# A gated recurrence with a small expert layer on one Trainium2 core: r and k of five early tiles loaded as two 48-row halves onto zeroed buffers

## The chip, the cores and the metric

The kernel runs on one core of a Trainium2 chip. The metric is the device time of one execution in microseconds. Three runs of the kernel before took 87.02, 87.03 and 86.26 us, median 87.02 us.

## The reference

Two layers follow each other. The first is a linear recurrence over 768 steps for 4 x 8 heads of dimension 48; the second is a mixture of eight low-rank experts with the two best chosen for each token, added to its input.

```python
batch, n_heads, seq, head_dim = (4, 8, 768, 48)
for t in range(S):
    cur = einsum('bhd,bhe->bhde', u * kt, vt)
    y[:, :, t] = einsum('bhd,bhde->bhe', rt, state + cur)
    state = wt[:, :, :, None] * state + einsum('bhd,bhe->bhde', kt, vt)

# x = y as (4*768, 384); E = 8 experts of rank 16, K = 2
logits = x @ w_gate
w = softmax over the two largest logits
delta = sum over the two chosen e of  w_e * ((x @ A[e]) @ B[e])
return x + delta
```

## The kernel before

The 768 steps of each batch entry are cut into 6 chunks of 128 (`L`), which gives 24 tiles (`NT`); a tile holds all eight heads of 128 steps. Heads go in pairs `p` (four pairs, `P`): on the 128 partitions one head of a pair has partitions 0 to 47 and the other 64 to 111, with the 48 channels of a head as rows and the 128 steps of each pair as columns.

Partitions 48 to 63 and 112 to 127 are left over by this. The host fills them with **doubled rows**: 16 channels each of the last pair's two heads, once in each of the first three pairs' blocks. The product r\*k for the term with `u` is therefore formed over three blocks (`PQ` = 3, 384 columns) and already holds all four pairs; three matmuls with the table `ub` (line 284, `dgmm`) sum it to one number for each step and head.

For one tile the steps are: `load_rk` (line 192) loads r and k of the tile in one transfer of 128 rows of 1028 f32 into one of 12 buffers `rks`; `load_w` loads the decays of two tiles (tiles 0 and 1 one each), `load_v` the values (the first three tiles through SP and a cast, `castv`; the later ones through POOL's queue, converted to bf16 on the way). `ln` (ACT) takes the logarithm of w, `cs` (PE) its running sum with a triangular matrix, `expp` and `expm` (ACT) the two exponentials. `qmul` (POOL) is r\*k, `rmul` (POOL) is r times the growing decay, `kmul` (DVE, for some tiles POOL) k times its inverse. `amm` (PE) forms the 128 x 128 products of each head, `aev` (DVE) masks them, `ktr`/`ktev` turn k, `kv`, `resc` and `sev` carry the state, `dgmm` and `dv` make the term with `u`, and `ymd`, `ymS`, `ymv` add the three parts of y. Every three tiles the gate runs (`zl`, `top`, `gexp`, `gsel`, `gmul`, `gnorm`, `gmul2`, `zw`, `zT`, `zTev`), and each tile ends with `dmm`, `oev` and `store`.

Nothing is scheduled automatically: the string `ORDER` (line 53) lists every step of every tile, and each engine executes its own steps in the order of that list. SP issues the plain loads and the stores in the order of the list, and a transfer that must wait holds all later ones back. The tuples above it (`K_ON_POOL`, `KT_ON_DVE`, `S_ON_DVE`, `Y_ON_DVE`, `OUT_ON_DVE`, `ZT_ON_ACT`, `CAST_ON_ACT`, `V_ON_ACT`) say which engine does a step for which tile. `warm.n` is n matmuls on zeros that keep PE occupied at the beginning. Ahead of the list DVE clears the padded buffers `lws` (four) and `dvs` (three), and POOL builds three constant matrices.

The list begins (line 54):

```python
warm.5 load_w.0 load_rk.0 ln.0 cs.0 warm.4 expp.0 expm.0 rmul.0 kmul.0 amm.0 warm.1 aev.0 qmul.0 load_w.1
ln.1 cs.1 warm.2 expp.1 expm.1 load_v.0 castv.0 consts.0 castc.0 dgmm.0 warm.2 dv.0 ymd.0 load_rk.1 qmul.1
rmul.1 kmul.1 load_w.2 ln.2 ktr.0 warm.2 ktev.0 cs.2 expp.2 expm.2 dgmm.1 load_v.1 castv.1 castv.2 dv.1
load_v.3 load_rk.2 qmul.2 rmul.2 kmul.2 load_rk.3 qmul.3 load_w.4 amm.1 aev.1 ymv.0 yev.0 ktr.1 ktev.1 kv.0
```

Tiles 6 to 8 stand in it on POOL as `qmul.6`, `rmul.6`, `qmul.7`, `load_v.9`, `qmul.8`, `rmul.7`, `kmul.7`, `qmul.9`.

Of the kernel before, what the change touches and what calls it, by code (L numbers as in the profile page):

```python
# [55 lines left out]
rmul.1 kmul.1 load_w.2 ln.2 ktr.0 warm.2 ktev.0 cs.2 expp.2 expm.2 dgmm.1 load_v.1 castv.1 castv.2 dv.1
load_v.3 load_rk.2 qmul.2 rmul.2 kmul.2 load_rk.3 qmul.3 load_w.4 amm.1 aev.1 ymv.0 yev.0 ktr.1 ktev.1 kv.0
warm.3 sev.0 cs.3 expp.3 expm.3 dgmm.2 load_v.6 kv.1 resc.1 sev.1 ln.4 ymd.1 ymS.1 ymv.1 yev.1 amm.2 warm.1
kmul.3 cs.4 expp.4 expm.4 dv.2 ymd.2 aev.2 rmul.3 ktr.2 ktev.2 consts.1 castc.1 load_rk.4 qmul.4 rmul.4
kmul.4 load_rk.5 load_w.6 load_rk.6 ymS.2 ymv.2 yev.2 amm.3 aev.3 kv.2 sev.2 dgmm.3 dv.3 cs.5 expp.5 expm.5  # L60
rmul.5 kmul.5 zl.2 top.2 gsel.2 consts.2 amm.4 warm.2 aev.4 ktr.3 ktev.3 ymd.3 ymS.3 ln.6 qmul.5 gexp.2
gmul.2 qmul.6 kv.3 resc.3 ymv.3 yev.3 dgmm.4 dv.4 sev.3 gnorm.2 gmul2.2 cs.6 expp.6 expm.6 rmul.6 amm.5
load_rk.7 qmul.7 load_w.8 load_rk.8 load_rk.9 load_w.10 load_rk.10 load_rk.11 load_w.12 load_rk.12
load_rk.13 load_w.14 ktr.4 ktev.4 ymd.4 ymS.4 ymv.4 yev.4 load_v.9 kv.4 sev.4 dgmm.5 qmul.8 load_rk.14
load_rk.15 kmul.6 cs.7 expp.7 expm.7 rmul.7 kmul.7 zw.2 zT.2 ln.8 castc.2 dv.5 ymd.5 dgmm.6 ymS.5 warm.1
# [10 lines left out]
dmm.6 oev.6 ymv.12 yev.12 kv.12 sev.12 rmul.13 kmul.13 amm.13 load_v.18 ktr.13 ktev.13 dmm.8 oev.8 qmul.15
load_w.16 load_rk.16 ln.16 qmul.16 load_rk.17 zl.11 kmul.14 cs.15 expp.15 aev.13 ymd.13 top.11 gexp.11
gsel.11 dgmm.14 dv.14 ymS.13 rmul.14 kv.13 resc.13 gmul.11 gnorm.11 expm.15 rmul.15 ymv.13 yev.13 amm.14
aev.14 sev.13 ktr.14 ktev.14 cs.16 ymd.14 ymS.14 dgmm.15 ymv.14 gmul2.11 zw.11 kv.14 zT.11 kmul.15 amm.15
dv.15 ktr.15 expp.16 expm.16 rmul.16 kmul.16 yev.14 ymd.15 qmul.17 zTev.11 cs.17 store.3 sev.14 ymS.15  # L80
aev.15 ktev.15 dgmm.16 dv.16 load_w.18 load_rk.18 ln.18 qmul.18 load_rk.19 dmm.10 oev.10 expp.17 rmul.17
expm.17 ymv.15 yev.15 kv.15 resc.15 sev.15 amm.16 ktr.16 ktev.16 cs.18 expp.18 expm.18 aev.16 store.5 zl.14
top.14 gexp.14 ymd.16 dgmm.17 dv.17 dmm.9 oev.9 ymS.16 kmul.17 amm.17 load_w.20 load_rk.20 load_rk.21
qmul.19 ymv.16 yev.16 kv.16 sev.16 gsel.14 ln.20 kmul.18 gmul.14 gnorm.14 gmul2.14 aev.17 dgmm.18 dmm.11
oev.11 cs.19 expp.19 expm.19 ymd.17 ymS.17 ymv.17 zw.14 zT.14 store.6 rmul.18 amm.18 zTev.14 qmul.20 store.7
dv.18 ktr.18 ktev.18 yev.17 aev.18 rmul.19 kmul.19 load_w.22 load_rk.22 load_rk.23 cs.20 ymd.18 dmm.13
oev.13 store.8 store.10 dgmm.19 dv.19 expp.20 expm.20 rmul.20 kmul.20 dmm.12 oev.12 qmul.21 kv.18 sev.18
ln.22 ymv.18 yev.18 zl.17 top.17 gexp.17 gsel.17 gmul.17 qmul.22 amm.19 aev.19 gnorm.17 gmul2.17 ktr.19
ktev.19 cs.21 expp.21 expm.21 kmul.21 dmm.14 oev.14 ymd.19 rmul.21 dgmm.20 dv.20 qmul.23 ymS.19 zw.17 ymv.19
yev.19 kv.19 resc.19 sev.19 amm.20 cs.22 store.13 zT.17 zTev.17 ymd.20 store.12 ktr.20 ktev.20 expp.22  # L90
# [13 lines left out]
def tile_kernel(ctx: ExitStack, tc: tile.TileContext, rk, w, v, ublk, aw, bm, out):  # L104
    nc = tc.nc
    nc.scalar.preload_act_table_set("natural_log_exp_and_others")
    const = ctx.enter_context(tc.tile_pool(name="const", bufs=1))
# [19 lines left out]
    lws = []  # L127
    for i in range(NLW):
        t_ = const.tile([128, WL, H, 64], FP16, name=f"lw{i}")
        nc.vector.memset(t_, 0.0)  # L130
# [60 lines left out]

    def load_rk(t):
        o = rks[t % RING]
        nc.sync.dma_start(out=o, in_=rk[t])
# [62 lines left out]
    def qmul(t):  # L257
        q = wk.tile([128, PQ, L], BF16, name="q", bufs=3)
        (nc.vector if t in Q_ON_DVE else nc.gpsimd).tensor_mul(q, st[t]["r"][:, 0:PQ], st[t]["k"][:, 0:PQ])  # L259
# [300 lines left out]
    stages = (warm, load_w, load_rk, load_v, castv, consts, castc, ln, cs, expp, expm, qmul, rmul, kmul, ktr, dgmm, ktev, dv, amm,  # L560
              aev, aev2, kv, resc, sev, ymd, ymS, ymv, ymv2, yev, yev2, zl, zl2, zx, nmax, top, gexp, gsel, gmul, gnorm, gmul2, zw, zT, zTev, pick, xev, dmm,
              oev, oev2, store, store2)
# [62 lines left out]
```

## Time and profile before

| | |
|---|---|
| three runs, median (lowest to highest) | 87.02 us (86.26 to 87.03) |
| the profiled execution, its own time | 86.5 us |
| its span, first to last instruction | 84.7 us |
| mean granted TensorE clock | 0.999 |
| moved by DMA | 25.43 MB, mean 300 GB/s |
| r and k of one tile | one transfer of 514.0 KB, median 10.1 us from issue to landing |

The profile describes one execution. Its page gives the busy time of each engine (PE for matmuls, PEld for their weight loads, DVE, ACT, POOL, and SP for issuing), then the span in 40 equal slices of 2.1 us with the busy tenths of each engine and the DMA engines' share and rate, then the chain of work that ended last, followed back from the end, and the costliest groups of instructions. In rows of the timeline the numbers are the start, the length, and in brackets the idle time of that engine just before, with what ended it. Lines such as L264 are lines of the kernel before.

### The profile page before, as it was taken

The numbers are of one execution on the slowest core, as the hardware profiler recorded it, in microseconds if no ns is written. First come the engines' busy times: TensorE is split into PE (matmuls) and PEld (weight loads), VectorE is DVE, ScalarE is ACT, GpSimd is POOL, SyncE is SP. The second block draws the span as 40 slices with busy tenths as digits, with TensorE's granted clock in tenths as the row PEclk, the third lists the DMA queues.
The fourth block names the chain that finished last, engine by engine and source line by source line (L and its number), as shares of the span: only waits on it lengthen the run. The fifth ranks groups of instructions, "written<-read, shape, count | busy, mean of one in ns | idle before, by whom it ended". The sixth has DMA issues, their size and how long they took to land.

```text
span 84.7 us, 3422 instructions
## 1 busy us (share of the span) xinstructions
PE 74.1 (88%) x1359; PEld 56.2 (66%) x1363; DVE 71.9 (85%) x174; ACT 68.4 (81%) x151; POOL 66.8 (79%) x95
## 2 busy tenths in 40 slices
PE   4899988997697999999999999999989999998610
PEld 1325666684476978688887978788768789675500
DVE  5947689968879999999999999999989986995730
ACT  6274689782899999999999999998999899956510
POOL 6059899969697999999999999997997996902000
PEclk9999999999999999999999999999999999999999
DMA  1999999999999999999999999999989004604261
GB/s 24 333 368 384 391 409 413 295 328 318 421 410 413 400 292 388 392 278 293 398 415 402 414 337 254 373 410 402 415 334 328 27 0 143 226 33 167 93 231 51
DMA packets 10384, 25.43 MB, mean 300 GB/s; under 512 B 1280, under 2 KB 4992, under 8 KB 10368
## 3 DMA queue, kind: packets, MB, share of 16 engines
q1 hardware_dynamic: 9648, 23.15, 71.1%
q0 software_dynamic: 720, 2.06, 12.3%
q8 instruction: 10, 0.16, 0.7%
q14 instruction: 6, 0.05, 0.2%
HBM read 22.56 MB, written 4.72 MB: 322 GB/s over the span
## 4 chain that ended last, share of the span: by engine, by line
DMA 39%; PE 27%; DVE 16%; ACT 4%; issue 3%; POOL 3%; SPq 1%; DVEq 0%; POOLq 0%
DMA rk<-in_rk_dram 15%; DMA out_dram<-res 10%; DMA aw_f<-in_aw_dram 9%; DMA v_f<-in_v_dram 5%; DVE at L315 5%; PE a_ps L308 4%; PE kd L282 3%; PE y_ps L365 3%; PE x_ps L241 2%; DVE dv L300 2%; PE d_ps L535 2%; PE y_ps L372 2%; PE d_ps L519 2%; PE z_ps L407 2%; PE y_ps L356 2%
## 5 line engine op out<-in xcount | busy, mean ns | idle before, releaser
L264 POOL TENSOR_TENSOR rd<-rk,ep 128x512 bf16<-128x512 f32 x24 | 26.1, 1089 | 3.6 <-ACT ep L249 2.8
L315 DVE TENSOR_TENSOR at<-a_ps,mask 128x1024 bf16<-128x1024 f32 x23 | 27.9, 1215 | 0.7 <-PE a_ps L308 0.6
L259 POOL TENSOR_TENSOR q<-rk 128x384 bf16<-128x384 f32 x24 | 20.6, 864 | 1.1 <-DMA rk<-in_rk_dram 0.9
L249 ACT ACTIVATE ep<-x_ps 128x512 f32<-128x512 f32 x24 | 14.7, 615 | 3.6 <-PE x_ps L243 2.1
L171 ACT CAST xT<-y_ps 128x512 bf16<-128x512 f32 x22 | 13.2, 598 | 2.1 <-PE y_ps L372 1.8
L241 PE MATMUL x_ps<-tri,lw 128*128 128x128 f16 x96 | 11.6, 223 | 1.4 <-ACT lw L231 1.4
L300 DVE TENSOR_TENSOR dv<-v_bf,kd 128x384 bf16<-128x384 bf16 x21 | 11.4, 544 | 1.2 <-DMA v_bf<-in_v_dram 1.1
L231 ACT ACTIVATE lw<-w_in 128x768 f16<-128x768 f32 (+1 forms) x13 | 10.5, 811 | 2.2 <-DMA w_in<-in_w_dram 2.2
L241 PEld LDWEIGHTS <-lw 128*128 128x128 f16 x96 | 7.7, 99 | 3.4 <-ACT lw L231 2.8
L356 PE MATMUL y_ps<-ident,dv 128*128 128x128 bf16 x94 | 9.2, 219 | 0.4 <-DVE dv L300 0.3
L171 ACT COPY ks<-kd 128x384 bf16<-128x384 bf16 x16 | 7.9, 496 | 1.6 <-DVE df L442 1.4
L165 PE MATMUL idle_ps<-zero 128*128 128x512 bf16 x19 | 7.3, 499 | 1.5 <-DVE zero L112 1.2
L171 ACT COPY res<-d_ps 128x384 f32<-128x384 f32 x17 | 8.3, 495 | 0.1
L372 PE MATMUL y_ps<-at,v_bf 128*48 128x128 bf16 x160 | 8.0, 221 | 0.1
L535 PE MATMUL d_ps<-b_b,zT 128*128 128x384 bf16 x24 | 7.8, 327 | 0.3 <-DVE zT L169 0.3
L365 PE MATMUL y_ps<-rd,sb 48*48 48x128 bf16 x156 | 8.0, 220 | 0.0
L255 ACT ACTIVATE x_ps<-x_ps 128x512 f32<-128x512 f32 x13 | 8.0, 616 | 0.0
L519 PE MATMUL d_ps<-ident,xT 128*128 128x96 bf16 x92 | 7.7, 206 | 0.0
L356 PEld LDWEIGHTS <-dv 128*128 128x128 bf16 x96 | 6.4, 98 | 1.4 <-DVE dv L300 1.2
L407 PE MATMUL z_ps<-aw_b,xT 128*128 128x136 bf16 x92 | 6.8, 223 | 0.4 <-ACT res L171 0.4
L255 ACT ACTIVATE em<-x_ps 128x512 f32<-128x512 f32 x11 | 6.7, 610 | 0.0
L243 PE MATMUL x_ps<-ones,lw 128*128 128x128 f16 x48 | 6.6, 219 | 0.0
(188 smaller groups left out, 162.8 us busy)
## 6 DMA issues: line engine op xcount, KB each, us to landing
rk<-in_rk_dram SPq DMA_DIRECT2D x24, 514.0 KB, 10.1
out_dram<-res SPq DMA_DIRECT2D x23, 192.0 KB, 3.0
w_in<-in_w_dram SPq DMA_DIRECT2D x11, 384.0 KB, 10.2
v_bf<-in_v_dram POOLq DMA_DIRECT2D x2, 576.0 KB, 9.1
v_bf<-in_v_dram POOLq DMA_DIRECT2D x3, 288.0 KB, 7.9
w_in<-in_w_dram SPq DMA_DIRECT2D x2, 192.0 KB, 3.3
v_f<-in_v_dram SPq DMA_DIRECT2D x1, 384.0 KB, 5.8
aw_f<-in_aw_dram SPq DMA_DIRECT2D x1, 272.0 KB, 7.7
```

What stands on the lines that cost most here:

```text
L171: nc.scalar.copy(out=o, in_=i)
L231: nc.scalar.activation(out=lw[:, o:o + n, :, 0:D].rearrange("p c h d -> p (c h) d"), in_=w_in[:, 0:n].rearrange("p c (h d) -> p (c h) d", ...
L241: nc.tensor.matmul(x_ps[:, p, :], lhsT=lwof(t, p), rhs=tri, start=True, stop=t % WL == 0)
L249: nc.scalar.activation(out=ep[:, :, o + 1:o + L + 1], in_=st[t]["x"], func=ACT.Exp)
L255: nc.scalar.activation(out=em, in_=st[t]["x"], func=ACT.Exp, scale=-1.0)
L259: (nc.vector if t in Q_ON_DVE else nc.gpsimd).tensor_mul(q, st[t]["r"][:, 0:PQ], st[t]["k"][:, 0:PQ])
L264: (nc.vector if t in R_ON_DVE else nc.gpsimd).tensor_mul(rd, st[t]["r"], st[t]["ep"][:, :, 0:L])
L300: nc.vector.tensor_mul(o[:, :, 0:D], vseq[t], dg.to_broadcast([128, H, D]))
L315: nc.vector.tensor_mul(at.rearrange("s g p f -> s (g p) f"), st[t]["a_ps"].rearrange("s g p f -> s (g p) f"), mask.to_broadcast([128, H, L]))
L356: nc.tensor.matmul(st[t]["y"][p], lhsT=st[t]["dv"][:, 2 * p:2 * p + 2, :].rearrange("p a b -> p (a b)"), rhs=ident, start=(p == 0 or (t == ...
L365: nc.tensor.matmul(st[t]["y"][p][s_], lhsT=st[t - 1]["sb"][s_, p, :], rhs=st[t]["rd"][s_, p, :], start=False, stop=False, skip_group_check ...
L372: nc.tensor.matmul(st[t]["y"][p][g * 64:g * 64 + D], lhsT=vseq[t][:, h, :], rhs=at, start=False, stop=(h >= H - 2 or (t == NT - 1 and h % ...
```

## The change

For tiles 1 to 5 (`EARLY`) r and k are loaded without the doubled rows: two transfers of 48 rows, to partitions 0 to 47 and 64 to 111. The rows between them are cleared once by a new step `rz` (a memset of the whole buffer, on POOL for tiles 1, 4 and 5, on DVE for 2 and 3), so that they hold zeros; the buffers are used again by tiles 13 to 17 with full rows. For these tiles `qmul` takes four blocks of 128 columns and `dgmm` four matmuls, with a second set of four blocks in the table `ub`. The memsets of `lws` and `dvs` become steps of the list (`lz`, `dz`). The casts of v for tiles 1 and 2 and of the table `aw` move from POOL to ACT, other steps change between DVE and ACT, and the whole list is planned anew.

```diff
-CAST_ON_ACT = (2,)
-V_ON_ACT = ()
+CAST_ON_ACT = (1, 2)
+V_ON_ACT = (1, 2)
+EARLY = (1, 2, 3, 4, 5)
+RZ_ON_POOL = (1, 4, 5)
 K_ON_POOL = (5, 7, 9, 11, 13, 15, 17, 19, 21, 22, 23)
-KT_ON_DVE = (0, 2, 9, 10)
-S_ON_DVE = (1, 3, 6)
-Y_ON_DVE = (17,)
-OUT_ON_DVE = (1, 6, 10, 13, 16, 19, 23)
-ZT_ON_ACT = (11, 14, 17, 20)
+KT_ON_DVE = (0, 2, 7, 10, 12, 18, 20)
+S_ON_DVE = (3, 15)
+Y_ON_DVE = ()
+OUT_ON_DVE = (1, 7, 16, 17, 23)
+ZT_ON_ACT = (8, 14, 17, 20)

 ORDER = """
+warm.5 load_w.0 lz.3 rz.1 load_rk.0 rz.4 lz.0 lz.1 load_w.1 ln.0 dz.2 rz.3 dz.1 dz.0 cs.0 warm.4 expp.0
+expm.0 rmul.0 kmul.0 amm.0 rz.5 rz.2 consts.0 qmul.0 lz.2 aev.0 castc.0 ln.1 cs.1 warm.2 expp.1 expm.1
+load_v.0 castv.0 dgmm.0 warm.3 dv.0 load_rk.1 qmul.1 kmul.1 load_w.2 ln.2 ktr.0 ymd.0 cs.2 load_v.1 castv.1
+expp.2 expm.2 ktev.0 kv.0 dgmm.1 warm.2 sev.0 castv.2 load_v.3 dv.1 ktr.1 ktev.1 rmul.1 amm.1 load_rk.2
+qmul.2 rmul.2 kmul.2 load_rk.3 load_w.4 load_v.6 aev.1 ymv.0 yev.0 cs.3 dgmm.2 dv.2 ymd.1 qmul.3 expp.3
+expm.3 rmul.3 kmul.3 ln.4 ymS.1 ymv.1 yev.1 kv.1 resc.1 sev.1 ktr.2 amm.2 cs.4 expp.4 expm.4 ymd.2 ymS.2
+consts.1 castc.1 aev.2 ymv.2 amm.3 yev.2 ktev.2 kv.2 sev.2 dgmm.3 load_rk.4 qmul.4 rmul.4 kmul.4 load_rk.5
+cs.5 qmul.5 expm.5 zl.2 aev.3 amm.4 dv.3 ktr.3 expp.5 top.2 gsel.2 ymd.3 ymS.3 aev.4 load_w.6 load_rk.6 ln.6
+cs.6 kmul.5 gexp.2 gmul.2 gnorm.2 ktev.3 dgmm.4 dv.4 expp.6 ymv.3 yev.3 kv.3 resc.3 sev.3 rmul.5 amm.5
+gmul2.2 zw.2 expm.6 kmul.6 ktr.4 ktev.4 qmul.6 rmul.6 load_v.9 ymd.4 ymS.4 dgmm.5 dv.5 load_rk.7 load_w.8
+load_rk.8 ln.8 qmul.8 ymv.4 yev.4 kv.4 sev.4 qmul.7 consts.2 cs.7 aev.5 zT.2 ymd.5 dgmm.6 ymS.5 expm.7 dv.6
+zTev.2 amm.6 aev.6 ymv.5 ktr.6 expp.7 rmul.7 cs.8 castc.2 dmm.1 oev.1 dmm.0 yev.5 ymd.6 ktev.6 dgmm.7 dv.7
...

     for i in range(NLW):
         t_ = const.tile([128, WL, H, 64], FP16, name=f"lw{i}")
-        nc.vector.memset(t_, 0.0)
         lws.append(t_)
...
         t_ = const.tile([128, H, 64], BF16, name=f"dv{i}")
-        nc.vector.memset(t_, 0.0)
...
-    ub_f = const.tile([128, PQ, H], F32, name="ub_f")
-    ub = const.tile([128, PQ, H], BF16, name="ub")
+    ub_f = const.tile([128, PQ + P, H], F32, name="ub_f")
+    ub = const.tile([128, PQ + P, H], BF16, name="ub")
...
+    def lz(i):
+        nc.vector.memset(lws[i], 0.0)
+
+    def dz(i):
+        nc.vector.memset(dvs[i], 0.0)
+
+    def rz(t):
+        (nc.gpsimd if t in RZ_ON_POOL else nc.vector).memset(rks[t], 0.0)
+
     def load_rk(t):
         o = rks[t % RING]
-        nc.sync.dma_start(out=o, in_=rk[t])
+        if t in EARLY:
+            for i in (0, 64):
+                nc.sync.dma_start(out=o[i:i + D], in_=rk[t, i:i + D])
+        else:
+            nc.sync.dma_start(out=o, in_=rk[t])
...
     def qmul(t):
-        q = wk.tile([128, PQ, L], BF16, name="q", bufs=3)
-        (nc.vector if t in Q_ON_DVE else nc.gpsimd).tensor_mul(q, st[t]["r"][:, 0:PQ], st[t]["k"][:, 0:PQ])
+        n = P if t in EARLY else PQ
+        q = wk.tile([128, P, L], BF16, name="q", bufs=3)[:, 0:n]
+        (nc.vector if t in Q_ON_DVE else nc.gpsimd).tensor_mul(q, st[t]["r"][:, 0:n], st[t]["k"][:, 0:n])
...
-        for p in range(PQ):
-            nc.tensor.matmul(dg, lhsT=st[t]["q"][:, p, :], rhs=ub[:, p, :], start=(p == 0), stop=(p == PQ - 1))
+        n, o = (P, PQ) if t in EARLY else (PQ, 0)
+        for p in range(n):
+            nc.tensor.matmul(dg, lhsT=st[t]["q"][:, p, :], rhs=ub[:, o + p, :], start=(p == 0), stop=(p == n - 1))
...
+    for j in range(H):
+        ublk[j % 2, 0:D, PQ + j // 2, j] = u[j]
```

More of the change, by code (lines that the diff above doesn't have):

```diff
@@ L56 @@
[L56 to L65, printed above, removed]
@@ L76 @@
[L76 to L85, printed above, removed]
@@ L86 @@
[L86 to L90, printed above, removed]
@@ new lines @@
+amm.12 aev.12 zT.8 rmul.13 qmul.14 expm.13 kmul.13 cs.14 ktr.12 ktev.12 yev.11 ymd.12 zTev.8 dmm.7 oev.7
+expp.14 expm.14 rmul.14 kmul.14 load_w.16 load_rk.16 ln.16 load_rk.17 load_w.18 load_rk.18 dmm.6 oev.6
+load_v.18 ymv.12 yev.12 kv.12 sev.12 dgmm.13 dv.13 qmul.16 zl.11 top.11 gexp.11 gsel.11 gmul.11 qmul.15
+store.5 amm.13 aev.13 ktr.13 ktev.13 cs.15 expp.15 expm.15 rmul.15 ymd.13 dmm.8 dgmm.14 dv.14 gnorm.11
+ymS.13 kv.13 oev.8 ymv.13 yev.13 store.3 resc.13 sev.13 amm.14 aev.14 ktr.14 ktev.14 store.4 cs.16 expp.16
@@ new lines @@
+expm.16 store.6 ymd.14 ymS.14 gmul2.11 zw.11 dgmm.15 dv.15 load_rk.19 load_w.20 load_rk.20 load_rk.21
+load_w.22 kmul.15 qmul.18 ymv.14 yev.14 kmul.16 store.7 kv.14 zT.11 zTev.11 store.8 ln.18 amm.15 aev.15
+ktr.15 ktev.15 rmul.16 ymd.15 cs.17 dmm.10 dgmm.16 dv.16 qmul.17 sev.14 kv.15 ymS.15 resc.15 sev.15 amm.16
+aev.16 expm.17 kmul.17 ymv.15 ktr.16 expp.17 cs.18 oev.10 zl.14 top.14 yev.15 ymd.16 ktev.16 dgmm.17 dv.17
+rmul.17 gsel.14 expp.18 expm.18 rmul.18 kmul.18 gexp.14 gmul.14 gnorm.14 gmul2.14 dmm.9 oev.9 store.10
@@ new lines @@
+load_rk.22 load_rk.23 qmul.19 ymS.16 kv.16 sev.16 ymv.16 yev.16 amm.17 aev.17 ln.20 dgmm.18 dv.18 qmul.21
+dmm.11 oev.11 store.11 cs.19 expp.19 expm.19 rmul.19 kmul.19 ymd.17 ymS.17 amm.18 ymv.17 yev.17 zw.14 ktr.18
+ktev.18 aev.18 zT.14 zTev.14 qmul.20 cs.20 expp.20 expm.20 rmul.20 dgmm.19 dv.19 ymd.18 kmul.20 dmm.13
+oev.13 store.13 dmm.12 oev.12 store.12 kv.18 sev.18 ymv.18 yev.18 amm.19 aev.19 ktr.19 zl.17 top.17 gsel.17
+cs.21 ymd.19 ktev.19 dgmm.20 dv.20 ln.22 qmul.22 ymS.19 gexp.17 gmul.17 gnorm.17 gmul2.17 expp.21 rmul.21
@@ L558, in store2 @@
         nc.sync.dma_start(out=out[t * 128:(t + 1) * 128, HD // 2:], in_=st[t]["res"][:, HD // 2:])
[L560 removed]
+    stages = (lz, dz, rz, warm, load_w, load_rk, load_v, castv, consts, castc, ln, cs, expp, expm, qmul, rmul, kmul, ktr, dgmm, ktev, dv, amm,
               aev, aev2, kv, resc, sev, ymd, ymS, ymv, ymv2, yev, yev2, zl, zl2, zx, nmax, top, gexp, gsel, gmul, gnorm, gmul2, zw, zT, zTev, pick, xev, dmm,
```

44 lines of the change are left out of this document (21 added, 23 removed).

## The prediction, made before the change was run

> **What bounds the kernel now.** I read the page first (shares, slices, chain, transfers), then the stages, then the chain in order of time, and last POOL's own timeline, because the page shows two different kernels in one: a beginning that waits for transfers and a long middle in which every engine is full.
>
> ```profile
> span 84.7 us, 3422 instructions
> PE 74.1 (88%) x1359; PEld 56.2 (66%) x1363; DVE 71.9 (85%) x174; ACT 68.4 (81%) x151; POOL 66.8 (79%) x95
> ...
> POOL 6059899969697999999999999997997996902000
> ...
> DMA  1999999999999999999999999999989004604261
> GB/s 24 333 368 384 391 409 413 295 328 318 421 410 413 400 292 388 392 278 293 398 415 402 414 337 254 373 410 402 415 334 328 27 0 143 226 33 167 93 231 51
> ...
> DMA 39%; PE 27%; DVE 16%; ACT 4%; issue 3%; POOL 3%; SPq 1%; DVEq 0%; POOLq 0%
> ```
>
> The 16 DMA engines are full from the second slice (2.1 us each) to about 64 us. POOL has holes up to slice 13 and none for long after it. The stages say the same in numbers; the columns are the length, then busy time of PE, PEld, DVE, ACT and POOL, the clock, the DMA share and GB/s.
>
> ```profile
> 5.00:10.00 5.00, 4.55 (x44) 2.18 (x42) 3.51 (x5) 2.98 (x6) 4.57 (x7) 1.00 1.01 390
> 10.00:27.00 17.00, 14.15 (x274) 10.74 (x275) 14.09 (x28) 13.41 (x28) 14.93 (x20) 1.00 1.04 375
> 27.00:57.00 30.00, 29.79 (x617) 24.67 (x613) 29.39 (x71) 29.61 (x69) 29.77 (x37) 1.00 1.04 361
> 57.00:75.00 18.00, 17.38 (x358) 14.03 (x351) 16.68 (x40) 15.95 (x39) 15.46 (x21) 1.00 0.61 226
> 75.00:84.70 9.70, 4.76 (x80) 3.33 (x74) 4.78 (x20) 4.04 (x11) 0.44 (x2) 0.99 0.35 123
> ```
>
> From 10 to 27 us DVE, ACT and POOL each lose 2 to 3.6 us; from 27 to 57 us none of them loses even 0.7 us. The chain and POOL's timeline (start, length, in brackets the idle time before and its releaser) show where the one regime turns into the other.
>
> ```profile
> 2.11 4.14 DMA v_f<-in_v_dram
> 6.27 7.73 DMA aw_f<-in_aw_dram
> 14.02 12.87 DMA rk<-in_rk_dram
> ```
>
> ```profile
> 5.14 1.09 POOL L264 TENSOR_TENSOR rd<-rk,ep 128x512 bf16<-128x512 f32 x1 [2.81 <-ACT ep L249]
> ...
> 23.01 0.86 POOL L259 TENSOR_TENSOR q<-rk 128x384 bf16<-128x384 f32 x1 [0.30 <-DMA rk<-in_rk_dram]
> ...
> 25.06 0.87 POOL L259 TENSOR_TENSOR q<-rk 128x384 bf16<-128x384 f32 x1
> ...
> 27.04 0.85 POOL L259 TENSOR_TENSOR q<-rk 128x384 bf16<-128x384 f32 x1 [0.58 <-DMA rk<-in_rk_dram]
> ...
> 73.25 1.09 POOL L269 TENSOR_TENSOR kd__2120<-rk,em 128x512 bf16<-128x512 f32 x1
> ```
>
> Up to 26.89 us (14.02 + 12.87) the chain is transfers alone: that last one is the load of r and k of tile 8, issued at 14.02 behind a full queue. The products q of tiles 6, 7 and 8 start at 23.01, 25.06 and 27.04; tiles 6 and 8 waited for their loads. From 27.04 to 74.34 (73.25 + 1.09) POOL then runs 47.3 us with little idle: none from 27 to 57, and in the stage from 57, of the 17.34 us up to 74.34, 17.34 - 15.46 = 1.9 us. So **the landing of tile 8's r and k sets the start of a POOL-bound stretch, and the end follows 57.7 us after it** (84.7 - 27.0). Whatever moves that landing moves the time about one for one.
>
> **The change, part by part.** *The loads.* Each of tiles 1 to 5 was one transfer of 128 rows of 4112 bytes; now it is two, of 48 rows each, to partitions 0 to 47 and 64 to 111.
>
> ```profile
> rk<-in_rk_dram SPq DMA_DIRECT2D x24, 514.0 KB, 10.1
> ...
> ub_f<-in_ublk_dram SPq DMA_DIRECT2D x1, 12.0 KB, 3.9
> ```
>
> A full load is 526 KB (514 x 1024), which at 390 GB/s (stage 5 to 10) is 1.35 us of a full queue. Two halves are 395 KB. No transfer in this trace covers fewer than 128 partitions, so the price of a half has to be bounded. *Low end:* time goes by bytes. Then a tile takes 1.01 us, saving 0.34, over five tiles **-1.7 us**. *High end:* time goes by the partitions reached, 48 of 128, so that a half takes as long as a whole (1.35): **+6.7 us**. *Between:* a half reaches one half of the partitions and gets half the rate, 197 KB at 195 GB/s, 1.01 us, 2.02 a tile, **+3.4 us** over five. The nearest rows are the full loads, and they show a rate only for full width: 384 to 421 GB/s in slices 4 to 7 and 11 to 13 of the page's row, all engines busy.
>
> ```profile
> 10.75 0.72 POOL L205 DMA_DIRECT2D v_bf<-in_v_dram  x1
> ...
> 14.18 0.59 POOL L205 DMA_DIRECT2D v_bf<-in_v_dram  x1
> ```
>
> In slices 8 to 10 (295, 328, 318), where the two loads of v issued here, which convert to bf16, share the engines, the engines are just as full while fewer bytes count. So an engine's time does not follow the bytes written into SBUF, which speaks a little for the low end, but says nothing of two engines writing into the same few partitions. I take the middle value, +3.4: with the halves issued one behind the other, the engines all work on the lower half and then all on the upper, and nothing in the order of transfers makes them do both at once. The larger ub table adds 16 KB, 0.04 us.
>
> On this the Trainium skill has a rule that speaks against the change. SBUF — State Buffer, section "Door 1: The DMA port swizzle (why `[64,N]` ≈ `[32,N]`)", says that partitions 0 to 63 reach only eight of sixteen ports, and gives 196 GB/s for 64 partitions against 328 for 128 at 1 MiB; its section "Can I just issue two DMAs to hit both halves?" says that two such transfers run one after the other (+6%). An estimate by that ratio of 0.6 is 0.84 us a half and +1.7 us over five tiles; by the port limits it gives, half the rate, it is the middle value again, and by bytes -1.7. No row of this trace shows it.
>
> *Zeroing.* Five memsets of 128x1028 f32 are new; those of lw and dv move from the start into the order.
>
> ```profile
> 1.38 2.11 DVE L130 MEMSET lw<- 128x512 uint32 x4
> ...
> 5.56 0.69 DVE L269 TENSOR_TENSOR kd__153<-rk,x_ps 128x512 bf16<-128x512 f32 x1 [1.00 <-ACT x_ps L255]
> 6.81 1.23 DVE L315 TENSOR_TENSOR at<-a_ps,mask 128x1024 bf16<-128x1024 f32 x1 [0.57 <-PE a_ps L308]
> ```
>
> ```profile
> 0.73 0.20 POOL masks.py:65 MEMSET tri<- 128x128 f16 x1 [0.29 <-POOLq L614]
> ```
>
> ```profile
> 0.74 0.38 SPq L188 DMA_DIRECT2D w_in<-in_w_dram  x1
> ...
> 4.49 1.01 SPq L194 DMA_DIRECT2D rk<-in_rk_dram x2
> ```
>
> DVE clears 512 elements in 0.53 us, so 1028 take 1.05; POOL, scaled from 128 elements in 0.20, takes at most 1.6 and, if half of that 0.20 is fixed, 0.9. Ahead of kmul.0 DVE gains one memset of r, k (tile 3) and loses one of lw: +0.5, inside the 1.00 us that it waited. Tiles 1 and 4 fall into POOL's 2.81 us of idle before rmul.0. Tile 2's (DVE, behind kmul.0) and lw 2's push the first mask product from 6.81 to about 7.8, and tile 5's (POOL) pushes q of tile 0 by 0.9 to 1.6; both lie ahead of the wait for loads, so I cost them at nothing; uncovered they are 1.0 and up to 1.6. Where SP waits: load_rk.2, issued at 4.49 before, must wait for tile 2's memset, to about 7.3, and rk.3, w.4, the aw table and rk.4 stand behind it on SP. What hides this is w.2 and v.1, which the queue still holds:
>
> ```profile
> 3.22 0.52 ACT L231 ACTIVATE lw<-w_in 128x384 f16<-128x384 f32 x1 [1.20 <-DMA w_in<-in_w_dram]
> ```
>
> ```profile
> 9.85 0.95 POOL L177 CAST v<-v_f 128x384 bf16<-128x384 f32 x2 [0.26 <-DMA v_f<-in_v_dram]
> ```
>
> v.1 landed at 9.85. The first transfer of all, w.0, was issued at 0.74 and used at 3.22, so that 2.5 us pass from issue to use and about 2 to the first bytes; from 7.3 that is 9.3, ahead of 9.85. Without that cover it would be up to 2.8 us. The five added issues are 0.3 to 0.5 us each (1.01 for two above) against 0.5 us and more of data per half.
>
> *r\*k over four blocks.* These five products go from 384 to 512 columns, the shape of rd, at L264.
>
> ```profile
> L264 POOL TENSOR_TENSOR rd<-rk,ep 128x512 bf16<-128x512 f32 x5 | 5.5, 1091 | 0.8 <-ACT em L255 0.7
> L259 POOL TENSOR_TENSOR q<-rk 128x384 bf16<-128x384 f32 x6 | 5.2, 865 | 0.3 <-DMA rk<-in_rk_dram 0.3
> ...
> L177 POOL CAST v<-v_f 128x384 bf16<-128x384 f32 x2 | 1.0, 504 | 0.3 <-DMA v_f<-in_v_dram 0.3
> L177 POOL CAST aw_b<-aw_f 128x544 bf16<-128x544 f32 x1 | 0.6, 637 | 0.0
> ```
>
> That is 5 x 0.23 = +1.1 us of POOL, and the casts of v 1, v 2 and aw, which go to ACT, take 1.6 off it; ACT had 3.6 us free between 10 and 27. PE gains five short matmuls, hidden. All of it lies before tile 8's landing: nothing.
>
> *The new order.* Up to tile 8 POOL's list is much alike, but q of tile 8 now stands **before** q of tile 7 (and r, k of tile 7). So 0.9 us that was done at 25.06, ahead of the landing, comes behind it: +0.9. Against that, while POOL stands waiting, ACT and DVE catch up, and DVE hands evictions to ACT (of its lists, three more of kT, one sb, one y and two out less); I let that remove half of the 1.9 us of late idle, -0.9 (bounds 0 and -1.9).
>
> *Sum.* Landing of tile 8: 26.9 + 3.4 = 30.3. Then 57.7 us to the end, +0.9 - 0.9: span 88.0. Around the span lie 1.8 us (86.5 of the profiled execution against 84.7), so **89.8 us**. The profiled 86.5 stands 0.5 below the median 87.02 and inside the runs (86.26 to 87.03).
>
> **The rivals.** *Time goes by bytes (the change does what its sizes say).* The landing moves to 25.2. POOL's work from rmul.0 (5.14) to q of tile 8 in the new order is eight products of 1.09 (seven rd, one kd), five q of 1.09 and two of 0.86, a memset of 1, two casts (0.7), three issues of v (1.9) and two gate products (0.5), 19 to 20 us, so it can be there at about 25 and meets the load; then 0.9 more work and 0 to 1.9 less idle: POOL ends 1 to 2 us earlier, and I take 1.1: span 83.6, **85.4 us**. For it: the converting loads above, and that 0.66 MB less (5 x 131 KB) pass ahead of tile 8. Against it: nothing shows 48-row transfers at the full rate.
>
> *The halves cost what a whole did.* If the engines drift apart enough for a lower half to overlap an upper one, the fullest partitions still take as many rows as before, and the landing stays at 26.9. Then only the order counts: +0.9 - 0.9, span 84.7, **86.5 us**, 86.0 to 87.4.
>
> *The queue runs dry behind the memset.* Should rk.2 wait for DVE beyond the end of v.1, the gap of up to 2.8 us goes straight into the landing: with loads by bytes, -1.7 + 2.8 = +1.1, **87.6 us**. Against it: the margin above.
>
> **How the numbers follow.** Halves slower than a whole (forecast; +1.0 to +6.7, own range 87.5 to 92.5): 0.57. Halves as a whole: 0.18. By bytes: 0.18. Dry queue: 0.07. Below 85.3 I leave about one tenth, the better part of the bytes case with a better plan; above 92.0 a tenth, the upper part of the full-width price. About 1% is what a measurement of this kernel can tell from no change. Faster by over 1% (under 86.15): 0.15 of the bytes case and 0.05 of a better plan with neutral loads, 0.20. Slower by over 1% (over 87.9): nearly all of the forecast, a third of the dry queue and some of the neutral case with a worse plan, 0.63. Within: 0.17.
>
> **What would show it.** Right: the GB/s row falls below 300 between about 6 and 20 us while the DMA share stays at 9 or more; r, k of tiles 2 to 5 land later than before though they are smaller; POOL's wait for tile 8's load before its q grows from 0.58 to 2 us or more, and q of tile 8 starts near 30; from there to the end are about 57 to 58 us. Wrong: GB/s stays near 390 and q of tile 8 starts by 26, or starts late after a wait that is not a load; or the stretch behind it changes by more than 1.5 us, which would make the plan and not the transfers the cause.

## The result, and the profile after

| | before | after |
|---|---|---|
| median (lowest to highest), 6 runs each | 87.03 us (85.99 to 87.41) | 91.14 us (90.99 to 93.52) |
| ratio, 95% interval | 1 | **1.0524** [1.0442, 1.0607] |
| profiled execution, span | 86.5 us, 84.7 us | 90.99 us, 89.2 us |

The change makes the kernel 4.1 us slower by the medians and 5.2% by the ratio. Ratios leave out executions that lie well above the rest of their kernel, so that they can differ a little from the quotient of two medians. The forecast was 89.8, in a range of 85.3 to 92.0.

The page after, in the lines that answer to those of before (busy time by engine, the 40 slices, now of 2.23 us, and the shares of the chain):

```profile
span 89.2 us, 3438 instructions
PE 76.6 (86%) x1360; PEld 58.1 (65%) x1361; DVE 72.9 (82%) x175; ACT 70.4 (79%) x155; POOL 69.0 (77%) x95
...
POOL 6839979905999899699999999997599799660000
PEclk9999999995559999999999999999999999999997
DMA  1999999999999999999999999999996522414343
GB/s 31 335 305 311 259 184 299 278 212 254 403 413 407 413 341 331 402 360 265 351 410 418 402 360 228 274 389 339 380 410 259 195 88 88 152 36 157 111 156 109
...
PE 29%; DMA 26%; POOL 17%; DVE 11%; issue 8%; SPq 3%; ACT 2%; POOLq 0%; DVEq 0%; ACTq 0%
```

The engines' busy sums rose by only 1.0 to 2.5 us. The GB/s row fell: slices 5 to 10 hold 184 to 299 where before none of slices 2 to 14 was below 295, and the DMA row beside it stays at 9. The transfers moved less while the 16 DMA engines were as full as ever. In the same place POOL falls to 0 in one slice, and the granted clock falls to half in slices 10 to 12.

Stages of the profile after (length, busy time of PE, PEld, DVE, ACT, POOL, clock, DMA share, GB/s):

```profile
5.00:10.00 5.00, 4.80 (x30) 2.35 (x29) 3.47 (x6) 2.71 (x6) 3.98 (x6) 1.00 0.98 302
10.00:27.00 17.00, 13.01 (x201) 9.78 (x202) 10.75 (x23) 11.45 (x24) 12.97 (x16) 0.80 1.05 290
...
29.21:89.20 59.99, 54.09 (x1086) 43.52 (x1081) 52.82 (x131) 52.19 (x121) 46.54 (x60) 0.99 0.79 275
```

From 10 to 27 us the rate fell from 375 to 290 GB/s at the same DMA share, and PE did 201 matmul instructions there instead of 274. POOL's own timeline shows where the transfers became a wait:

```profile
12.83 1.09 POOL L274 TENSOR_TENSOR q<-rk 128x512 bf16<-128x512 f32 x1 [0.54 <-DMA rk<-in_rk_dram]
...
21.11 1.09 POOL L274 TENSOR_TENSOR q<-rk 128x512 bf16<-128x512 f32 x1 [3.44 <-DMA rk<-in_rk_dram]
...
29.21 1.70 POOL L274 TENSOR_TENSOR q<-rk 128x384 bf16<-128x384 f32 x2
...
64.44 0.86 POOL L274 TENSOR_TENSOR q<-rk 128x384 bf16<-128x384 f32 x1 [0.91 <-DMA rk<-in_rk_dram]
```

The second row is q of tile 4. It waits 3.44 us for its load; in the profile of before the same product came without a wait:

```profile
16.42 0.86 POOL L259 TENSOR_TENSOR q<-rk 128x384 bf16<-128x384 f32 x1
...
19.07 1.09 POOL L264 TENSOR_TENSOR rd<-rk,ep 128x512 bf16<-128x512 f32 x1 [0.74 <-ACT em L255]
...
22.47 0.23 POOL L475 TENSOR_TENSOR pe<-sel,ge 128x24 f32<-128x24 f32 x1 [0.44 <-ACT ge L455]
```

At tile 4 POOL is thus 4.7 us late (21.11 - 16.42), about as much as the end (89.2 - 84.7 = 4.5). The delay is not simply carried there, though: q of tile 8 starts only 2.2 us later than before (29.21 against 27.04), and 2.3 us more are lost behind it. Between these two products POOL stood idle for 2.1 us before (0.74, 0.44, and the 0.30 and 0.58 ahead of q of tiles 6 and 8) and not at all after, and q of tile 7 has moved behind q of tile 8. The chain of waits, in order of time:

```profile
6.46 0.69 DVE kd__157 L284
7.31 0.93 DVE rk L200
8.25 0.33 SPq L206
...
11.03 0.38 SPq L206
11.44 9.45 DMA rk<-in_rk_dram
21.11 0.37 POOL q L274
...
54.04 10.28 DMA rk<-in_rk_dram
```

The end hangs on tile 2's memset on DVE (L200), on SP's issues behind it, and on the load of tile 4, issued at 11.44 and 9.45 us on its way; then, late, on the load of tile 21, issued at 54.04, for which the q at 64.44 waits.

### The profile page after: what moved, and what is told of

It is laid out like the page before. It is cut to its first block, busy times and chain, and to the rows that moved or that the text cites. A ratio compares the mean times of both kernels' runs of the same rounds, so it can differ in the third digit from the quotient of the medians.

```text
span 89.2 us, 3438 instructions
## 1 busy us (share of the span) xinstructions
PE 76.6 (86%) x1360; PEld 58.1 (65%) x1361; DVE 72.9 (82%) x175; ACT 70.4 (79%) x155; POOL 69.0 (77%) x95
## 4 chain that ended last, share of the span: by engine, by line
PE 29%; DMA 26%; POOL 17%; DVE 11%; issue 8%; SPq 3%; ACT 2%; POOLq 0%; DVEq 0%; ACTq 0%
DMA rk<-in_rk_dram 22%; POOL rd L279 6%; POOL q L274 6%; PE a_ps L324 4%; DMA w_in<-in_w_dram 4%; PE y_ps L388 3%; PE d_ps L551 3%; PE x_ps L255 3%; DVE at L331 3%; PE d_ps L535 3%; PE z_ps L423 3%; PE kd L297 2%; PE y_ps L381 2%; SPq L206 2%; PE y_ps L372 2%
## 5 line engine op out<-in xcount | busy, mean ns | idle before, releaser
L274 POOL TENSOR_TENSOR q<-rk 128x384 bf16<-128x384 f32 (+1 forms) x24 | 21.8, 912 | 5.0 <-DMA rk<-in_rk_dram 4.9
L255 PE MATMUL x_ps<-tri,lw 128*128 128x128 f16 x96 | 12.5, 234 | 4.7 <-DVE kd__431 L284 3.2
L171 ACT CAST xT<-y_ps 128x512 bf16<-128x512 f32 x23 | 13.7, 597 | 0.6 <-PE y_ps L388 0.2
L255 PEld LDWEIGHTS <-lw 128*128 128x128 f16 x96 | 8.1, 104 | 3.6 <-ACT lw L245 2.5
L171 ACT COPY res<-d_ps 128x384 f32<-128x384 f32 x19 | 9.0, 485 | 0.9 <-PE d_ps L551 0.8
L165 PE MATMUL idle_ps<-zero 128*128 128x512 bf16 x15 | 6.5, 568 | 1.3 <-DVE zero L114 1.2
L423 PE MATMUL z_ps<-aw_b,xT 128*128 128x136 bf16 x92 | 7.5, 235 | 0.0
L257 PE MATMUL x_ps<-ones,lw 128*128 128x128 f16 x48 | 7.4, 235 | 0.0
L171 ACT COPY ks<-kd 128x384 bf16<-128x384 bf16 x13 | 6.3, 484 | 1.3 <-PE kd L297 1.3
L257 PEld LDWEIGHTS <-lw 128*128 128x128 f16 x48 | 5.0, 105 | 3.4 <-issue 3.3
```

What stands on the lines that cost most here:

```text
L171: nc.scalar.copy(out=o, in_=i)
L255: nc.tensor.matmul(x_ps[:, p, :], lhsT=lwof(t, p), rhs=tri, start=True, stop=t % WL == 0)
L257: nc.tensor.matmul(x_ps[:, p, :], lhsT=lwof(t - 1, p), rhs=ones, start=False, stop=True)
```

## The experiments

Each kernel ran beside the kernel before on the same chip, and its ratio is to that one.

**The price of a half, by itself.** Only transfers, in stages of 8 or 12 tiles, each stage behind a memset of one column of every buffer; 132.41 us in all.

```diff
+    def rows(i, a, b, eng=None):
+        (eng or nc.sync).dma_start(out=bufs[i][a:b], in_=rk[i, a:b])
...
+        for i in range(8): nc.sync.dma_start(out=bufs[i], in_=rk[i])
+        for i in range(8): rows(i, 0, D); rows(i, 64, 64 + D)
+        for i in range(8): rows(i, 0, 64); rows(i, 64, 128)
+        for i in range(12): rows(i, 32, 96)
+        for i in range(12): rows(i, 40, 88)
+        for i in range(12): rows(i, 0, 48)
+        for i in range(8): rows(i, 0, D); rows(i, 64, 64 + D, nc.scalar)
+        for i in range(8): rows(i, 0, 112)
```

> Loads of r and k alone, nothing of the reference is computed; eight stages with a full stop between them: (1) 8 whole tiles of 128 rows; (2) 8 tiles as rows 0 to 47, then 64 to 111; (3) 8 tiles as rows 0 to 63, then 64 to 127; (4) 12 times rows 32 to 95; (5) 12 times rows 40 to 87; (6) 12 times rows 0 to 47; (7) as 2, but the upper half issued by ACT beside SP; (8) 8 times rows 0 to 111 in one transfer. If a rate follows the groups of partitions a transfer reaches (lower and upper half apart): 1 near 400 GB/s, 2, 3 and 6 near 200, 4 and 5 well over 300 though they are as small, 7 between (over 300 if the two halves pass side by side). If it is the size or the number of transfers that costs: 4 and 5 as slow as 3 and 6. If time goes by bytes: all near 400.

The stages ran into one another at their ends, so only the spacing of landings inside a stage is read. A memset of 128x1 follows each landing; its start is the landing. Two rows from each of seven stages, in the order whole loads, the change's halves, halves of 64, rows 32 to 95, rows 40 to 87, rows 0 to 47, and last rows 0 to 111:

```profile
21.27 0.06 DVE L124 MEMSET b<- 128x1 f32 x1 [1.23 <-DMA b<-in_rk_dram]
22.55 0.06 DVE L124 MEMSET b<- 128x1 f32 x1 [1.22 <-DMA b<-in_rk_dram]
...
31.24 0.06 DVE L124 MEMSET b<- 128x1 f32 x1 [1.90 <-DMA b<-in_rk_dram]
33.21 0.06 DVE L124 MEMSET b<- 128x1 f32 x1 [1.91 <-DMA b<-in_rk_dram]
...
47.05 0.06 DVE L124 MEMSET b<- 128x1 f32 x1 [2.04 <-DMA b<-in_rk_dram]
49.18 0.06 DVE L124 MEMSET b<- 128x1 f32 x1 [2.08 <-DMA b<-in_rk_dram]
...
59.33 0.06 DVE L124 MEMSET b<- 128x1 f32 x1 [0.58 <-DMA b<-in_rk_dram]
59.97 0.06 DVE L124 MEMSET b<- 128x1 f32 x1 [0.58 <-DMA b<-in_rk_dram]
...
67.74 0.06 DVE L124 MEMSET b<- 128x1 f32 x1 [0.62 <-DMA b<-in_rk_dram]
68.44 0.06 DVE L124 MEMSET b<- 128x1 f32 x1 [0.64 <-DMA b<-in_rk_dram]
...
77.25 0.06 DVE L124 MEMSET b<- 128x1 f32 x1 [1.23 <-DMA b<-in_rk_dram]
78.54 0.06 DVE L124 MEMSET b<- 128x1 f32 x1 [1.23 <-DMA b<-in_rk_dram]
...
109.74 0.06 DVE L124 MEMSET b<- 128x1 f32 x1 [1.77 <-DMA b<-in_rk_dram]
111.57 0.06 DVE L124 MEMSET b<- 128x1 f32 x1 [1.77 <-DMA b<-in_rk_dram]
```

| rows of a tile | KB | us from landing to landing | GB/s worked out |
|---|---|---|---|
| 0-127 | 526 | 1.28 | 411 |
| **0-47 and 64-111, as in the change** | 395 | **1.97** | 200 |
| 0-63 and 64-127 | 526 | 2.13 | 247 |
| 32-95 | 263 | 0.64 | 411 |
| 40-87 | 197 | 0.70 | 282 |
| 0-47 | 197 | 1.29 | 153 |
| 0-111, one transfer | 461 | 1.83 | 252 |

A tile in halves takes 0.69 us more than a whole one, 3.5 us over five tiles, while it moves a quarter less; over its stage the spacing runs from 1.87 to 1.98 us, so that 3 us is the low end. A single half of 48 rows at 0 to 47 takes as long as all 128 rows. Twelve transfers of rows 32 to 95, as small as a half of 64, went at the full rate, so neither the size nor the number of transfers makes the halves slow, but which rows they reach. Halves issued by SP and ACT, whose upper rows ran beside the stage before, moved 187 to 237 GB/s, no better than two halves from SP; that stage settles nothing more.

**The halves inside the kernel.** The changed kernel with whole loads for tiles 1 to 5, memsets and wider products kept:

```diff
-            for i in (0, 64):
-                nc.sync.dma_start(out=o[i:i + D], in_=rk[t, i:i + D])
+            nc.sync.dma_start(out=o, in_=rk[t])
```

> The changed kernel with one edit: r and k of tiles 1 to 5 come in one transfer of 128 rows each, as before the change; plan, memsets and r*k over four blocks stay. Theory 1 (the 48-row halves run at about half the rate and delay all that lands behind them): the transfers of the first 28 us go back to about 375 to 400 GB/s, POOL's 3.4 us wait for tile 4 falls below 0.7 us, time 86.0 to 87.8 us. Rival (the new plan, the memsets and the wider products make the loss): 89.5 us or more, the wait turning up elsewhere.

It took 89.39 us, 1.0276 [1.016, 1.0393], between the two forecasts. From 10 to 27 us the rate went back to 362 GB/s, but POOL's wait for tile 4, which I had expected below 0.7 us, was still 2.46:

```profile
19.07 1.09 POOL L273 TENSOR_TENSOR q<-rk 128x512 bf16<-128x512 f32 x1 [2.46 <-DMA rk<-in_rk_dram]
```

The halves therefore cost 1.0524 - 1.0276 = 2.5%, 2.2 us (the intervals allow about 1 to 3.4), and about half of the loss stays without them. The opposite edit, halves of 64 rows that carry all bytes:

```diff
-                nc.sync.dma_start(out=o[i:i + D], in_=rk[t, i:i + D])
+                nc.sync.dma_start(out=o[i:i + 64], in_=rk[t, i:i + 64])
```

> The changed kernel with halves of 64 rows (partitions 0 to 63 and 64 to 127), so that all bytes of a whole load move, in two transfers that reach half of the partitions each. If a transfer's rate follows the partitions it reaches: no faster than the 48-row halves, 90.5 to 94 us. If time goes by bytes and it is the odd row count (48) or something of that kind that costs: as the whole loads, 86 to 88 us.

It took 93.67 us, 1.0776 [1.0675, 1.0876]. Splitting a load of the same bytes costs 5.0% (1.0776 - 1.0276); POOL's waits for r and k show it, from the list of waits (total, times, longest) of the kernel with whole loads, of the one with 64-row halves, and of the change:

```profile
POOL q L273 <- DMA rk<-in_rk_dram: 2.8, 2, 2.5
```

```profile
POOL q L274 <- DMA rk<-in_rk_dram: 8.4, 5, 4.7
```

```profile
POOL q L274 <- DMA rk<-in_rk_dram: 4.9, 3, 3.4
```

2.8 us with whole loads, 8.4 with all bytes in halves, 4.9 with the change's halves. It is the split at row 64 that costs, and the bytes that the change saves give back only a part.

**The plan alone.** The new order and lists, whole loads, no memsets of r and k, and r*k over three blocks:

```diff
-EARLY = (1, 2, 3, 4, 5)
+EARLY = ()
...
-        (nc.gpsimd if t in RZ_ON_POOL else nc.vector).memset(rks[t], 0.0)
+        return
```

> The changed kernel with the new plan alone: whole loads, three blocks of r*k, no memsets of the r, k buffers. Theory 1: the plan by itself costs within 0.8 us of nothing, 86.0 to 87.8 us. Rival: the plan loses, 89 us or more.

It took 87.8 us, 1.0116 [1.0039, 1.0192]: the plan, which I had costed at nothing, loses about 1 us. Its profile has a late wait of POOL ahead of q of tile 21:

```profile
58.69 0.87 POOL L274 TENSOR_TENSOR q<-rk 128x384 bf16<-128x384 f32 x1
60.90 0.86 POOL L274 TENSOR_TENSOR q<-rk 128x384 bf16<-128x384 f32 x1 [1.34 <-PE zT_ps L522]
```

The new order puts `qmul.21` in front of `rmul.19` and `kmul.19`. The releaser named is PE's zT, which q does not read; in the profile of the change the same wait is put down to the load (0.91 us at 64.44). So I moved only that:

```diff
-ymS.16 kv.16 sev.16 ymv.16 yev.16 amm.17 aev.17 ln.20 dgmm.18 dv.18 qmul.21 dmm.11 oev.11 store.11
-cs.19 expp.19 expm.19 rmul.19 kmul.19 ymd.17
+ymS.16 kv.16 sev.16 ymv.16 yev.16 amm.17 aev.17 ln.20 dgmm.18 dv.18 dmm.11 oev.11 store.11
+cs.19 expp.19 expm.19 rmul.19 kmul.19 qmul.21 ymd.17
```

> The new plan alone (whole loads, three blocks, no memsets of the r, k buffers), with one step moved: r*k of tile 21 from ahead of the two POOL products of tile 19 to behind them. In the plan-alone run POOL stood 1.3 us before it at 60.9 us, and PE then 1.3 us for kd of tile 19. If this wait for tile 21's load is what the plan loses: 1 us less than the 87.8 of the plan alone, 86.3 to 87.1 us. Rival (the loss lies in the early part and is only passed on): 87.5 us or more.

87.58 us, 1.0065 [1.0018, 1.0112]: about half of the plan's loss is gone by the middle values, though the two intervals overlap. I had expected 86.3 to 87.1, so this is not the whole cause. The late wait itself has left the timeline:

```profile
60.89 1.09 POOL L278 TENSOR_TENSOR rd<-rk,ep 128x512 bf16<-128x512 f32 x1 [0.39 <-ACT ep L262]
61.95 1.09 POOL L283 TENSOR_TENSOR kd__1731<-rk,em 128x512 bf16<-128x512 f32 x1
62.99 1.69 POOL L273 TENSOR_TENSOR q<-rk 128x384 bf16<-128x384 f32 x2
```

**The rest of the change under the old plan.** The kernel before, with its order and lists, plus the five memsets, the wider products and the halves; and the same with whole loads. The memsets stand where the change has them:

```diff
-warm.5 load_w.0 load_rk.0 ln.0 cs.0 warm.4 expp.0 expm.0 rmul.0 kmul.0 amm.0 warm.1 aev.0
+warm.5 load_w.0 rz.1 load_rk.0 rz.4 ln.0 rz.3 cs.0 warm.4 expp.0 expm.0 rmul.0 kmul.0 amm.0 warm.1 rz.5 rz.2 aev.0
```

> The kernel before, with its own plan, and only the halves put in: two 48-row transfers for tiles 1 to 5, their memsets where the new plan has them, r*k of these over four blocks. Theory 1: the halves cost in the old plan as much as in the new, 89.5 to 92 us. Rival (the old plan would have carried the halves): 88 us or less.

> The kernel before with its own plan, the memsets and four blocks of r*k for tiles 1 to 5, but whole loads of 128 rows; against the same with halves (89.5 us) the difference is the price of the halves in the old plan. By the spacing of the loads alone (1.97 us for a tile in halves, 1.27 whole) 3.5 us less at most. Theory 1 (the halves are nearly all of the loss): 86.2 to 87.3 us. Rival (memsets and wider products cost as much): 88 us or more.

With halves 89.49 us, 1.0325 [1.0253, 1.0396]; with whole loads 87.93, 1.0089 [1.0046, 1.0131]. So under the old plan the halves cost 2.4%, 2.0 us, and the memsets with the wider products 0.8 us, less than the halves but not nothing. The halves do not need the new plan to lose. In the old plan the 10 to 27 us stage with halves reads:

```profile
10.00:27.00 17.00, 14.89 (x271) 10.94 (x270) 13.05 (x28) 12.33 (x25) 15.66 (x20) 1.00 1.05 309
```

309 GB/s in place of 375, a fall as in the change (290), but the clock stays at 1.00 and PE does 271 matmul instructions.

**An earlier memset.** With whole loads the DMA engines go half dry once; this is the view of the first 28 us (slices of 0.7 us) of the kernel with whole loads and the new plan:

```profile
DMA  0039999999995999999999999999999999999999
GB/s 0 0 66 350 394 328 339 426 379 397 373 398 139 329 388 358 368 380 319 347 307 280 283 368 353 335 276 291 315 408 425 405 405 428 418 400 438 395 376 429
```

In the slice from 8.4 us the rate is 139, shortly after SP came past tile 2's memset. I moved that memset to POOL, ahead of rd of tile 0, once with halves and once with whole loads:

```diff
-RZ_ON_POOL = (1, 4, 5)
+RZ_ON_POOL = (1, 2, 4, 5)
...
-warm.5 load_w.0 lz.3 rz.1 load_rk.0 rz.4 lz.0
+warm.5 load_w.0 lz.3 rz.1 load_rk.0 rz.4 rz.2 lz.0
...
-expm.0 rmul.0 kmul.0 amm.0 rz.5 rz.2 consts.0
+expm.0 rmul.0 kmul.0 amm.0 rz.5 consts.0
```

> The changed kernel with tile 2's memset moved from DVE behind kmul.0 to POOL's idle time ahead of rmul.0, so that SP need not stop for it (2.9 us in the changed kernel). Theory 1 (the DMA engines were full all the time, so a later issue cost nothing there): 90.4 to 91.5 us, as changed. Rival (the stop of SP is the loss): 89.4 us or less.

> The same with whole loads of 128 rows for tiles 1 to 5. With whole loads the DMA engines ran dry for a slice while SP stood waiting for that memset; if this is what the memsets cost (87.8 us for the plan alone, 89.4 with memsets and wider products): 87.3 to 88.4 us, and the difference to the halves with the same early memset is the price of the halves, which I forecast at 3.4 us. Rival (the wider products and the memsets' own time on the engines): 88.9 us or more.

With halves 91.04 us, 1.0383 [1.0313, 1.0453]: SP issues tile 2's load at 5.11 us in place of 8.25, and the ratio lies 1.2 us below the change's 1.0524, but the two intervals touch and the median says no gain; not clear. With whole loads 90.49, 1.0273 [1.022, 1.0327]: the same ratio as with the late memset (1.0276). My theory there, that the half-dry slice was what whole loads lose, expected 87.3 to 88.4 us and fell. The difference for which the two were run, 1.0383 - 1.0273 = 1.1%, puts the halves at 1.0 us (by the intervals 0.2 to 1.7) once the memset is early, about half of the 2.2 with the late one. So a part of what the halves cost in the new plan may hang on SP's stop; the intervals also allow that it does not.

**The clock.** In the change PE stands 3.2 us at tile 4, and its granted clock falls to half. Thirteen filler matmuls behind dgmm.3 were to bridge the wait. The change itself ran beside the second filler run as a control:

```diff
-yev.2 ktev.2 kv.2 sev.2 dgmm.3 load_rk.4
+yev.2 ktev.2 kv.2 sev.2 dgmm.3 warm.13 load_rk.4
```

> The changed kernel with 13 filler matmuls on PE in the 3.2 us in which it waits for tile 4's k, after which its granted clock stood at about half for some 5 us. Theory 1 (the loss is in the loads; the clock is an aftermath that costs little): 90.2 to 91.2 us. Rival (the clock is a main part of the loss): 89.3 us or less.

> The changed kernel with the 13 filler matmuls again, now beside the changed kernel itself and with more rounds. Theory A (the drop of the granted clock after PE's 3.2 us of waiting costs a part of the loss, as the first look hinted): 1 to 2 us below the changed kernel. Theory B (the first look was scatter between runs): within 0.5 us of it.

> The changed kernel unaltered, beside the next three on one chip. All theories: 90.5 to 91.5 us.

The filler gave 90.57 us, 1.0256 [1.0181, 1.0331], and again 91.5, 1.0442 [1.0342, 1.0541]; the control 91.96, 1.0538 [1.0447, 1.0629], which repeats the change's 1.0524. The first time the median fits theory 1, but the ratio, 89.2 us beside its own kernel before, fits the rival, and its interval lies clear below the change's, by 2.3 us in the middle. The second time, beside the control on the same chip, the gain is 0.8 us with overlapping intervals, between theories A and B. The mean clock was 0.95 to 1.00 in the ten executions with the filler and 0.92 to 0.96 in the twelve of the change. The filler held the clock in the first profile (mean 0.99); in the second (0.95) it had fallen to half at about 13.4 us, long before the filler at 21.85. The plan alone has such a drop as well, and no profile of the old order has one, so that a part of the plan's 1.0 us may be the clock. It probably has a share in the loss, but this edit is no clean test, and how large the share is stays open.

## Why the prediction was right, and where it was not

The direction held, and so did the cause that it rests on: the halves are slower than a whole load, on engines that stay full. They are about half of the loss; the other terms were mis-sized. The kernels split the loss like this (1% is 0.87 us; the parts of the new plan add up because each is the difference to the next kernel):

| term | forecast, us | new plan, us | old plan, us |
|---|---|---|---|
| halves | +3.4 | +2.2 (1.0524 - 1.0276) | +2.0 (1.0325 - 1.0089) |
| memsets, wider r\*k | 0 | +1.4 (1.0276 - 1.0116) | +0.8 (1.0089 - 1) |
| new order and lists | 0 | +1.0 (1.0116 - 1) | none |
| sum | +3.4 | +4.6 | +2.8 |

The intervals behind these are wide: under the new plan 0.9 to 3.4, 0.2 to 2.6 and 0.3 to 1.7 us, under the old 1.3 to 2.8 for the halves. With tile 2's memset moved early the halves came to 1.0 us instead of 2.2.

*The halves' own time.* Forecast 0.67 us a tile, measured 0.69 with loads alone. That the two are so close is luck, for the picture was wrong: I let a half run at half the rate, 1.01 us. Alone it takes 1.29 us, and two behind each other 1.97, not 2.58, because they overlap in part. The high end of the bounds (a half as long as a whole) holds for one half, the overlap then brings the pair near the middle. *Time goes by bytes* fell: 1.97 where it asked for 1.01. *Halves as a whole* fell as well, by the same row.

*One for one into the end.* This step failed in size. Of 3.5 us in the transfers only 2.0 to 2.2 reach the end, 1.0 with the early memset. Two reasons can be read from the rows, though no run isolates them: before, the products of tiles 2 to 5 came after their loads had landed (q of tile 4 started at 16.42 with no wait), and a later landing eats that slack first; and POOL's 2.1 us of idle time between tiles 4 and 8 took up a part of the rest.

*The place.* I expected the wait at tile 8, with q of tile 8 near 30 behind a wait of 2 us or more. q of tile 8 started at 29.21, without a wait: POOL was still busy with what tile 4 had held up, and the wait (3.44 us) stood at tile 4. The load that POOL waits for longest is now one of the tiles that are loaded in halves.

*The new order.* The +0.9 came: POOL's busy time from q of tile 8 to the end is 46.54 us where the same stretch before had 45.67.

```profile
27.04:84.70 57.66, 51.88 (x1039) 42.01 (x1036) 50.82 (x128) 49.56 (x117) 45.67 (x59) 1.00 0.79 279
```

The -0.9 did not: POOL's idle time there went from 57.66 - 45.67 = 12.0 to 59.99 - 46.54 = 13.5 us, up 1.5 where I had it shrink. I judged a hand-over of evictions by what it takes off DVE, which by my own count (three more, four less) is one, and did not ask what each moved q waits for; q of tile 21 was put ahead of work that was ready, and waited 0.91 us for its load. The stretch thus came out at 60.0 us, 2.3 over the 57.7 of before, more than the 1.5 that I had set as the mark that the plan has a share in the cause. It has: 1.0 us by the run of the plan alone.

*Zeroing and wider products at nothing.* That failed too: 0.8 us [0.4, 1.1] under the old plan, 1.4 under the new. I named w.2 and v.1 as the cover for SP's stop, and bounded it at 2.8 us if uncovered. SP came to tile 2's load at 8.25 us in the change, later than the 7.3 that I had worked out. The half-dry slice shows this cover to be short where the loads are whole, but the earlier memset did not bring the loss back there, so the stop is not shown to be its cause; with halves it may be a part. Left are the 1.1 us of wider products on POOL, which I called hidden, and the memsets themselves: 0.93 us on DVE (tile 2's, in the chain above), and the same on POOL, here two in the profile after:

```profile
2.27 1.85 POOL L200 MEMSET rk<- 128x1028 f32 x2
```

No run takes these apart. Single profiles can't either: q of tile 4 starts 1.4 us apart with the plan alone and with q of tile 21 moved, though both have the same work up to there:

```profile
17.32 0.87 POOL L274 TENSOR_TENSOR q<-rk 128x384 bf16<-128x384 f32 x1 [1.34 <-PE y_ps L388]
```

```profile
18.76 0.86 POOL L273 TENSOR_TENSOR q<-rk 128x384 bf16<-128x384 f32 x1 [2.49 <-DMA rk<-in_rk_dram]
```

The errors offset each other: a transfer term that was too large by 1.2 us against two terms of 1.0 and 1.4 us that I had set to nothing. That the sum came out near is in part luck. The median came out 1.3 us above the forecast; 0.5 of that is the start from the profiled 86.5 in place of the median 87.0, the rest what the errors leave. One bound was added up wrongly: the forecast's own range would end at 86.5 + 6.7 = 93.2, not at 92.5.

## What to carry to other kernels

Before trimming rows off a load to save bytes, time the trimmed shape by itself: here a quarter fewer bytes took half again as long, and the sign could be read from seven stages of transfers in one run. A load that is made slower ahead of a full pipeline costs less than its own added time where the consumers had slack, so look for the first consumer without it, which need not be the one that bound before. In a list written by hand, check each moved instruction for what it waits on and what ready work stands behind it on its engine; one early product seems to have cost here about half of what the whole new order lost.
